# Filler matmuls in the head of a SwiGLU kernel: from two groups to three

## The chip, the cores and the metric

The kernel runs on one core of a Trainium2 chip. The metric is device time in microseconds (us) of one execution; a median of several is quoted, with the lowest and highest. "Span" is the time from the first to the last instruction in a profile; it is 1.3 to 1.4 us shorter than the device time of the same execution throughout.

## The reference

```python
B, S, D, F = 1, 2048, 640, 1536          # bf16
def reference(x, w_gate, w_up, w_down):
    g = silu(x @ w_gate)
    u = x @ w_up
    return (g * u) @ w_down
```

## The kernel before

The 2048 rows of x are done in four blocks of 512. For each block and each of twelve 128-wide slices of F, TensorE makes a gate projection `pg` and an up projection `pu`; ScalarE and VectorE make silu(pg)·pu; then the down projection follows. The first block needs x transposed, and this is done on TensorE, chunk by chunk (128 rows each, five transposes), in the order 0, 2, 1, 3. Chunks 0 and 2 are the first x pieces on the two DMA queues, 1 and 3 the second.

TensorE's matmuls follow each other slowly at first and about twice as fast later: in the profile before, 128 columns take 107 ns up to 3.47 us and 56 ns from 4.48 us on. I call this a low clock and the full one, although the column of the granted clock reads 1.00 throughout. With no fillers at all the change came at 7.0 to 7.4 us (the first experiment below). So the kernel fills TensorE with matmuls of ones ("fillers", into a tile `pw` that nobody reads) while it has nothing else to do:

```python
N_WARM = 20
W_CHUNKS = [(0, 1), (1, 3), (3, 6), (6, 9), (9, 12)]   # slices of F per weight load
...
for c in (0, 1):                                        # x: first pieces 0, 2; second 1, 3
    for i, eng in enumerate(queues):                    # queues: SyncE, ScalarE
        load_x(eng, c + 2 * i, c + 2 * i + 1)
for dst, src in ((wg_sb, wg_v), (wu_sb, wu_v)):         # then slice 0 of gate and up
    ...
load_w(nc.sync, wg_sb, wg_v, *W_CHUNKS[1])              # then slices 1 and 2, and so on
...
def warm(n):
    for _ in range(n):
        nc.tensor.matmul(pw[:, 0:P], lhsT=ones[:], rhs=ones[:], start=True, stop=True)
...
if sb == 0 and fc == 0:
    h = (SUB - 1) * P
    warm(N_WARM)
    for n, c in enumerate((0, 2, 1)):
        transpose_chunk(c, [(nc.vector.tensor_copy, ("po_a", "po_b")[n % 2], 0, KD)])
    transpose_chunk(SUB - 1, [...])                     # chunk 3: copies on VectorE and ScalarE
    warm(2)
    proj(pg, wg_sb, fc, sb, 0, h)                       # chunks 0 to 2: needs copy of chunk 1
    proj(pg, wg_sb, fc, sb, h, S_BLK)
    proj(pu, wu_sb, fc, sb, 0, S_BLK)
    keep_order(mybir.EngineType.PE)                     # TensorE keeps this order
```

## Time and profile before

| what | value |
|---|---|
| median of the first three runs | 164.19 us (164.17 to 164.63) |
| span of the profiled execution | 163.1 us (its device time: 164.41 us) |
| TensorE busy | 159.1 us, 98% |
| fillers | 22, 2.6 us busy |
| first gate matmul | 5.39 us after the start |

The lines themselves stand in the prediction. Two habits of reading matter here. A matmul's record is longer than its turn: most fillers have records of 311 ns and start 107 ns apart. What counts is the step from start to start. For 128 columns it is 107 ns at the low clock and 56 ns at the full one. And the moment at which the step changes is what I call the release of the clock.

### The profile page before, as it was taken

How to read it: one execution, taken by the hardware profiler on the slowest of the kernel's cores; microseconds unless marked ns; L12 is line 12 of the kernel's file. 1: busy time of each engine (PE TensorE's matmuls, PEld its weight loads, DVE VectorE, ACT ScalarE, POOL GpSimd, SP SyncE). 2: the span in 40 equal slices, each digit the busy share in tenths (PEclk: the TensorE clock that was granted, in tenths of full speed). 3: DMA queues.
4: the chain of work that ended last, by engine and by line, in shares of the span. 5: the costliest groups of instructions: out<-in, count | busy, mean ns of one | idle time of the engine just before them, and what ended most of it. 6: DMA issues, size and time to landing. Idle time of an engine off the chain costs nothing.

```text
span 163.1 us, 1864 instructions
## 1 busy us (share of the span) xinstructions
PE 159.1 (98%) x764; PEld 75.2 (46%) x779; DVE 37.8 (23%) x58; ACT 42.2 (26%) x71; POOL 0.6 (0%) x6
## 2 busy tenths in 40 slices
PE   8899999999999999999999999999999999999994
PEld 7544444444444444444444444444444444445442
DVE  2323333310013333311003333331001333332000
ACT  3222222212232222221222222221214222222121
POOL 1000000000000000000000000000000000000000
DMA  7999999803200000003110000000320000000312
GB/s 212 274 333 330 361 245 187 152 6 60 67 32 0 0 0 0 4 0 34 64 64 0 2 4 0 0 0 3 62 68 32 0 0 0 0 0 4 54 34 72
DMA packets 26888, 11.26 MB, mean 69 GB/s; under 512 B 17664, under 2 KB 26880, under 8 KB 26880
## 3 DMA queue, kind: packets, MB, share of 16 engines
q1 hardware_dynamic: 17968, 10.16, 22.9%
q10 hardware_dynamic: 8912, 0.98, 3.9%
q8 instruction: 6, 0.10, 0.3%
q14 instruction: 2, 0.02, 0.0%
HBM read 6.55 MB, written 2.62 MB: 56 GB/s over the span
## 4 chain that ended last, share of the span: by engine, by line
PE 95%; DMA 2%; issue 1%; DVE 0%; SPq 0%
PE pg L134 32%; PE pu L134 31%; PE po_a L204 25%; PE po_t L180 6%; DMA x_sb<-in_x_dram 2%; PE po_b L217 0%; PE pt L125 0%; DVE xT L130 0%; SPq L74 0%; DVE ot_b L225 0%
## 5 line engine op out<-in xcount | busy, mean ns | idle before, releaser
L134 PE MATMUL pg<-xT,wg_sb 128*128 128x512 bf16 (+2 forms) x245 | 59.7, 375 | 0.2 <-DVE xT L130 0.2
L134 PE MATMUL pu<-xT,wu_sb 128*128 128x512 bf16 x230 | 59.0, 379 | 0.5
L172 DVE TENSOR_TENSOR aT<-sg,pu 128x512 bf16<-128x512 f32 x48 | 33.0, 687 | 100.8 <-PE pu L134 100.8
L171 ACT ACTIVATE sg<-pg 128x512 f32<-128x512 f32 x48 | 28.7, 597 | 71.1 <-PE pg L134 71.1
L204 PE MATMUL po_a<-wd_sb,aT 128*128 128x512 bf16 x188 | 41.9, 379 | 0.2
L134 PEld LDWEIGHTS <-wg_sb 128*128 128x128 bf16 x245 | 23.8, 98 | 28.4 <-DMA wg_sb<-in_w_gate_dram 0.4
L134 PEld LDWEIGHTS <-wu_sb 128*128 128x128 bf16 x240 | 23.4, 98 | 28.1
L204 PEld LDWEIGHTS <-aT 128*128 128x128 bf16 x192 | 18.8, 98 | 22.5
L212 ACT CAST ot<-po_a 128x512 bf16<-128x512 f32 x16 | 9.4, 585 | 32.4 <-PE po_a L204 19.2
L180 PE MATMUL po_t<-aT,wd_sb 128*128 128x512 bf16 (+1 forms) x47 | 10.3, 366 | 0.1
L180 PEld LDWEIGHTS <-wd_sb 128*128 128x128 bf16 x48 | 4.7, 98 | 5.1
L189 ACT CAST ot_t<-po_t 128x512 bf16<-128x512 f32 (+1 forms) x4 | 2.2, 558 | 11.6 <-PE po_t L180 11.6
L190 DVE STREAM_TRANSPOSE ot_q<-ot_t 128x512 bf16<-128x512 bf16 (+1 forms) x4 | 2.7, 678 | 9.1 <-ACT ot_t L189 9.1
L103 PE MATMUL pw<-ones 128*128 128x128 bf16 x22 | 2.6, 302 | 0.4 <-DVE ones L78 0.4
L225 DVE CAST ot_b<-po_b 128x128 bf16<-128x128 f32 x1 | 0.3, 292 | 9.9 <-PE po_b L217 9.9
L125 PE MATMUL pt<-ident,x_sb 128*128 128x128 bf16 x20 | 2.0, 269 | 0.5 <-DMA x_sb<-in_x_dram 0.5
L130 DVE COPY xT<-pt 128x640 bf16<-128x640 bf16 (+1 forms) x4 | 1.7, 439 | 3.5 <-PE pt L125 3.5
L103 PEld LDWEIGHTS <-ones 128*128 128x128 bf16 x22 | 2.2, 139 | 0.4 <-DVE ones L78 0.4
L125 PEld LDWEIGHTS <-x_sb 128*128 128x128 bf16 x20 | 1.6, 122 | 0.9 <-DMA x_sb<-in_x_dram 0.8
L89 ACT ACT_TABLE_LOAD x1 | 1.3, 1283 | 2.0 <-issue 2.0
L130 ACT COPY xT<-pt 128x384 bf16<-128x384 bf16 x1 | 0.5, 479 | 1.6 <-PE pt L125 1.6
L217 PEld LDWEIGHTS <-aT 128*128 128x128 bf16 x12 | 0.8, 98 | 0.2
(9 smaller groups left out, 2.1 us busy)
## 6 DMA issues: line engine op xcount, KB each, us to landing
out_dram<-ot SPq DMA_DIRECT2D x16, 128.0 KB, 1.7
wd_sb<-in_w_down_dram SPq DMA_DIRECT2D x1, 1920.0 KB, 11.8
wg_sb<-in_w_gate_dram SPq DMA_DIRECT2D x3, 480.0 KB, 7.1
wu_sb<-in_w_up_dram SPq DMA_DIRECT2D x3, 480.0 KB, 7.8
out_dram<-ot_q ACTq DMA_DIRECT2D x12, 32.0 KB, 1.9
x_sb<-in_x_dram SPq DMA_DIRECT2D x2, 160.0 KB, 3.1
x_sb<-in_x_dram ACTq DMA_DIRECT2D x2, 160.0 KB, 3.3
wg_sb<-in_w_gate_dram SPq DMA_DIRECT2D x1, 320.0 KB, 4.3
```

Of the source, the lines that this page charges most:

```text
L89: nc.scalar.activation(silu_first[:], ones[:, 0:1], ACT.Silu)
L103: nc.tensor.matmul(pw[:, 0:P], lhsT=ones[:], rhs=ones[:], start=True, stop=True)
L125: nc.tensor.transpose(out=pt[:, kd - k0, :], in_=x_sb[:, c, kd * P : (kd + 1) * P], identity=ident[:],)
L130: copy(out=xT[:, k0:k1, c_sl], in_=pt[:])
L134: nc.tensor.matmul(ps[:, c0:c1], lhsT=w_sb[:, kd, fc * P : (fc + 1) * P], rhs=xT[:, kd, sb * S_BLK + c0 : sb * S_BLK + c1], start=(kd == 0 ...
L171: nc.scalar.activation(sg[:], pg[:], ACT.Silu)
L172: nc.vector.tensor_tensor(out=aT[:, fc, s_sl], in0=sg[:], in1=pu[:], op=ALU.mult)
L180: nc.tensor.matmul(po_t[:], lhsT=wd_sb[:, kf, DA:D], rhs=aT[:, kf, sb * S_BLK : sb * S_BLK + n_t], start=(kf == 0), stop=(kf == KF - 1),)
L189: nc.scalar.copy(ot_t[:], po_t[:])
L190: nc.vector.transpose(out=ot_q[:], in_=ot_t[:])
L204: nc.tensor.matmul(po_a[:], lhsT=aT[:, kf, s0 : s0 + P], rhs=wd_sb[:, kf, 0:DA], start=(kf == 0), stop=(kf == KF - 1),)
L212: nc.scalar.copy(ot[:], po_a[:])
```

## The change

Its intent: spread the fillers over the head so that TensorE is kept busy in its holes too. Two fewer at the front, four new ones between the two pairs of x pieces, and four instead of two before the gate projection.

```diff
-    N_WARM = 20
+    N_WARM, N_GAP = 18, 4
@@
                     transpose_chunk(
                         c, [(nc.vector.tensor_copy, ("po_a", "po_b")[n % 2], 0, KD)]
                     )
+                    if c == 2:
+                        warm(N_GAP)
@@
-                warm(2)
+                warm(N_GAP)
                 proj(pg, wg_sb, fc, sb, 0, h)
```

## The prediction

> **What bounds the kernel now.** I read four things, in this order: the page for the whole, the chain of waits over the first 10 us for the head, the timeline of the head for the gaps on TensorE, and the table of stretches for how much of each gap is idle.
>
> The page first. Its slices, its chain and the group of the fillers:
>
> ```profile
> PE   8899999999999999999999999999999999999994
> PE 95%; DMA 2%; issue 1%; DVE 0%; SPq 0%
> L103 PE MATMUL pw<-ones 128*128 128x128 bf16 x22 | 2.6, 302 | 0.4 <-DVE ones L78 0.4
> ```
>
> TensorE is busy in every slice except the first two and the last, and 95% of the chain that ends last is its matmuls. The change touches nothing but the first slices (40 slices over 163.1 us are 4.08 us each), so whatever it does must happen before about 6 us. The fillers are 22 matmuls of ones, 2.6 us busy in all. The only other engine in this chain worth a per cent is the DMA, 2% of 163.1 us, or some 3.3 us, and that is at the head.
>
> The chain of waits over the first 10 us, in order of time, says which thing in the head is on the path:
>
> ```profile
> 0.46 3.81 DMA x_sb<-in_x_dram
> 4.26 0.05 issue
> 4.31 0.51 PE pt L125 x5
> 4.82 0.02 issue
> 4.84 0.50 DVE xT L130
> 5.35 0.04 issue
> 5.39 1.25 PE pg L134 x10
> ```
>
> The reader is to see that no filler is in it, and neither is the first half of x. The path is: the last of the second x pieces lands at 4.26, its five transposes take 0.51, VectorE copies them in 0.50, and the gate projection starts at 5.39. After that TensorE runs without a gap that matters.
>
> The timeline of the head shows where the fillers stand beside that path (start, length, engine, line, what):
>
> ```profile
> 0.40 2.31 PE L103 MATMUL pw<-ones 128*128 128x128 bf16 x20 [0.40 <-DVE ones L78]
> 2.51 1.27 PE L125 MATMUL pt<-ident,x_sb 128*128 128x128 bf16 x10
> 4.31 0.78 PE L125 MATMUL pt<-ident,x_sb 128*128 128x128 bf16 x10 [0.53 <-DMA x_sb<-in_x_dram]
> 4.92 0.27 PE L103 MATMUL pw<-ones 128*128 128x128 bf16 x2
> 5.37 1.09 PEld L134 LDWEIGHTS <-wg_sb 128*128 128x128 bf16 x10 [0.35 <-DMA wg_sb<-in_w_gate_dram]
> 5.39 1.25 PE L134 MATMUL pg<-xT,wg_sb 128*128 128x384 bf16 x10 [0.19 <-DVE xT L130]
> ```
>
> There are two holes: 0.53 us before the second x pieces, and 0.19 us before the gate projection. The gate projection has two releasers close together: its weight load was let go by the landing of the gate slice, at 5.37, and its first matmul by VectorE's copy, at 5.39. Removing one of the two would leave the other.
>
> These lines also hold the clock. A matmul's record runs on past the start of the next by its pipeline, so I take the step from start to start. Twenty fillers in 2.31 us with a last record of 0.31 us (the source view of their line gives 311 ns as the median) make 2.00/19 = 105 ns a step. The last two fillers, 0.27 us with a last record of 0.22, step by about 55 ns. The single records of the transposes say when this changes: they step by 107 ns up to 3.47, and by 80, 87 and then 56 ns from 4.31 on. So in this execution the clock was released between about 4.3 and 4.5 us, just as the second x pieces came, and before the gate projection. The column of the granted clock reads 1.00 throughout and doesn't show it.
>
> Last, the table of stretches, cut at the joints of the head, gives the idle share:
>
> ```profile
> 3.57:4.30 0.73, 0.21 (x2) 0.00 (x0) 0.69 (x2) 0.00 (x0) 0.00 (x0) 1.00 1.02 230
> 5.03:5.38 0.35, 0.17 (x3) 0.01 (x1) 0.35 (x2) 0.26 (x1) 0.00 (x0) 1.00 0.96 267
> ```
>
> In the first stretch TensorE started nothing; the 0.21 us is the tail of two earlier records. So counted by starts the first hole is 0.73 us and the second 0.35 us. The DMA column is full: the transfers are what is waited for.
>
> [...]the x pieces here took 2.5 to 3.9 us from issue to landing (the tile view of x_sb)[...].
>
> **The change part by part.**
>
> First, two fillers fewer at the front. They would end 2 x 0.107 = 0.21 us earlier, so that TensorE could take the first transpose at 2.51 - 0.21 = 2.30. But the landings in the trace have the last part of the first x piece at 2.46, and the first weight load from x started at 2.50, 0.10 later than it would have behind a filler. It waited for the landing already. So the first transposes stay at 2.50 and a gap of 0.2 us opens ahead of them: 0.00 us on the path.
>
> Second, four fillers after the first two chunks. The last of those ten transposes starts at 3.47, so the fillers start at 3.57 and at the slow step take 4 x 0.107 = 0.43 us, to 4.00. The second pieces land at 4.26. There is 0.26 us to spare, and no filler takes a buffer that the transposes need (pw is its own tile, and they wait for no other engine): 0.00 us on the path. Were the clock released in this hole they would be shorter still.
>
> Third, four instead of two before the gate projection: two more, at the released step 2 x 0.056 = 0.11 us. The transposes' slots end at 4.92, and four fillers to 5.15. The gate slice's landing lets the load go at 5.37, the copy lets the matmul go at 5.39: 0.22 us to spare, and 0.00 us on the path.
>
> Sum in the state of the traced execution: 0.00. TensorE does four matmuls more, 26 against 22, all in holes. If anything comes of the change, it comes through the clock[...].
>
> **The rivals.**
>
> (a) The clock is released earlier, or more surely. For it: in the traced execution the release comes just at the edge where it begins to matter[...]. In executions with a later release, five transposes at 107 instead of about 60 ns a step put the copy, and so the gate projection, some 0.2 to 0.25 us later, and each microsecond of projections at half clock costs 0.5 us more. That is the size of the 164.63 us run, 0.45 us above the others. Against it: two of three runs lie at 164.18, and those have nothing to win[...]. If only the late executions win, the median stays; if all had a part, some 0.2 us, it would be 164.0.
>
> (b) The fillers get in the way. In an execution where the clock is still slow at 5 us, ten transposes from 4.31 end their slots at 4.31 + 10 x 0.107 = 5.38, two fillers bring it to 5.59 and four to 5.81. The copy would release the gate projection at about 4.31 + 4 x 0.107 + 0.31 + 0.05 + 0.49 + 0.05 = 5.65. So two fillers hide, and four delay it by 0.16 us. For it: nothing shows that such executions are rare. [...]It would make 164.35 of a late execution's 164.19, if one had that time, and hardly move the median.
>
> (c) The transfers move. Weights for the second slice land at 7.19 and their first load starts at 7.34, so even a head that was 0.2 us faster would meet this wait after 0.15 us. This caps any win. The DMA issues themselves stay in their order on SyncE and ScalarE; the landing of the second x pieces was set by one late part of sixteen (fifteen had landed by 3.29, the last at 4.26), which can well differ by some tenths between executions, with the change or without.
>
> **Range and chances.** I give 0.7 to no effect (164.19), 0.2 to (a) in a form that the median shows (164.0), 0.1 to (b) (164.35). The mean is 164.17, and as the last case is mostly hidden by a median I say 164.15 us. The spread of the kernel before, 0.46 us in three runs, is wider than all of this, so the range is set by it: 163.90 (the whole cap of (c) and some luck with the landings) to 164.60 (a median caught in the late state). Two per cent is 3.3 us, nearly the whole time before the second x pieces land; no part of the change reaches that either way. Faster 0.01, within 2% 0.98, slower 0.01.
>
> **What would show it.** In the profile after: 18 fillers, then the first transposes still at about 2.5 with a wait for x_sb now named ahead of them; four fillers at about 3.6 that end their slots at about 4.0; the idle time before the second transposes cut from 0.53 to some 0.1 us and still put down to the x transfer; four fillers at about 4.9; the gate projection released by VectorE's copy or the gate slice, within 0.2 us of 5.39 after correction for the landing. It would be wrong if the transposes of the second pieces start later than 0.1 us after their landing, if the gate projection follows a filler without a gap, or if the gate projection starts over 0.3 us earlier at the same landing, which would mean that the clock had been on the path in most executions.

Cut from the recorded text is what no trace or run of this case shows: a section on when the clock is released, two arguments of (a) and one of (b) about the same, a remark on the transfers of x, and the end of the paragraph on the sum. The forecast stands without them. Its sum is 0.00 us on the path, from three parts of 0.00 us each, and its time comes from the three chances: 0.7 x 164.19 + 0.2 x 164.0 + 0.1 x 164.35 = 164.17 us, said as 164.15. The term cut from the sum was a count of idle time, 0.43 + 0.11 - 0.21 = 0.33 us less of it on TensorE, and that this moves the release was not shown. The 0.5 us for each microsecond of projections at the low clock is my estimate, from the steps of 107 and 56 ns.

## The result

The kernel after took 164.23 us in the median of six runs (163.98 to 164.82), beside 164.28 us (164.16 to 164.63) for six of the kernel before. The ratio of the two is 0.9997, with a 95% interval of 0.9976 to 1.0018: the same. A ratio here is the mean time of one kernel's fast runs over that of the other's of the same rounds, so it is not quite the ratio of the medians.

The profile after tells a less smooth story, for it caught the slowest of the six, at 164.82 us. From its page, the chain by engine and the group of the fillers:

```profile
PE 96%; DMA 2%; issue 1%; SPq 0%; DVE 0%
L103 PE MATMUL pw<-ones 128*128 128x128 bf16 x26 | 3.2, 304 | 0.4 <-DVE ones L78 0.4
```

Four fillers more, as the diff says, 26 of them. From the chain of waits in the first 10 us of the kernel after (start, length, what; its ends are left out):

```profile
0.46 3.91 DMA x_sb<-in_x_dram
4.37 0.04 issue
4.41 1.25 PE pt L125 x10
5.66 0.28 PE pw L103 x4
5.93 1.09 PE pg L134 x10
```

Here a filler is in the chain: the gate projection follows ten transposes and four fillers without a wait. The timeline of TensorE in the same execution (start, length, what, and in brackets the idle time before it):

```profile
0.40 2.10 PE L103 MATMUL pw<-ones 128*128 128x128 bf16 x18 [0.40 <-DVE ones L78]
2.45 1.25 PE L125 MATMUL pt<-ident,x_sb 128*128 128x128 bf16 x10
3.49 0.63 PE L103 MATMUL pw<-ones 128*128 128x128 bf16 x4
4.41 1.25 PE L125 MATMUL pt<-ident,x_sb 128*128 128x128 bf16 x10 [0.29 <-DMA x_sb<-in_x_dram]
5.45 0.48 PE L103 MATMUL pw<-ones 128*128 128x128 bf16 x4
5.77 1.25 PE L134 MATMUL pg<-xT,wg_sb 128*128 128x384 bf16 x10
```

The second ten transposes take 1.25 us, where they took 0.78 us before: they ran at the low clock. The single records put the release between 5.5 and 5.7 us, over a microsecond later than in the profile before (4.3 to 4.5). The gate projection starts at 5.77 instead of 5.39 us, and the span is 163.5 instead of 163.1 us: the same 0.4 us. The table of stretches confirms that the holes were filled (length, then TensorE's busy time):

```profile
3.57:4.30 0.73, 0.55 (x6) 0.29 (x3) 0.61 (x2) 0.00 (x0) 0.00 (x0) 1.00 1.25 283
5.03:5.38 0.35, 0.35 (x6) 0.35 (x5) 0.22 (x1) 0.00 (x0) 0.00 (x0) 1.00 1.06 271
```

So the fillers did what they were placed for, TensorE was busier (0.21 to 0.55 us, and 0.17 to 0.35 us), and this execution was released later all the same. Is that the change, or chance? That is what the experiments had to tell.

### The profile page after: what moved, and what is told of

It reads as the page before. It is cut to its first block, busy times and chain, and to the rows that moved or that the text cites. A ratio compares the mean times of both kernels' runs of the same rounds, so it can differ in the third digit from the quotient of the medians.

```text
span 163.5 us, 1872 instructions
## 1 busy us (share of the span) xinstructions
PE 159.9 (98%) x768; PEld 76.0 (46%) x783; DVE 37.9 (23%) x58; ACT 42.2 (26%) x71; POOL 0.6 (0%) x6
## 4 chain that ended last, share of the span: by engine, by line
PE 96%; DMA 2%; issue 1%; SPq 0%; DVE 0%
PE pg L134 32%; PE pu L134 31%; PE po_a L206 25%; PE po_t L182 6%; DMA x_sb<-in_x_dram 2%; PE pt L125 1%; PE po_b L219 0%; SPq L74 0%; DVE ot_b L227 0%; PE pw L103 0%
## 5 line engine op out<-in xcount | busy, mean ns | idle before, releaser
L103 PE MATMUL pw<-ones 128*128 128x128 bf16 x26 | 3.2, 304 | 0.4 <-DVE ones L78 0.4
L103 PEld LDWEIGHTS <-ones 128*128 128x128 bf16 x26 | 2.7, 145 | 0.4 <-DVE ones L78 0.4
L125 PE MATMUL pt<-ident,x_sb 128*128 128x128 bf16 x20 | 2.5, 311 | 0.3 <-DMA x_sb<-in_x_dram 0.3
```

The lines of the kernel that those rows point to most:

```text
L125: nc.tensor.transpose(out=pt[:, kd - k0, :], in_=x_sb[:, c, kd * P : (kd + 1) * P], identity=ident[:],)
```

## The experiments

**Theory:** The fillers at the front are what brings the release forward; those in the holes neither move it nor the path, and what differs between executions is the moment of release and the landings. **Rival (a):** the busy time in the holes makes the release earlier or surer. **Rival (b):** fillers in the holes stand in TensorE's order ahead of real work and cost. All variants below but one, the wide slices, change only the three counts, written (front, first hole, before the gate projection): the kernel before is (20, 0, 2), the kernel after (18, 4, 4). Each was timed six times beside eleven runs of the kernel before; each group of four has its own chip, so a variant is compared with the kernel before of its own group. Those had medians of 164.26, 164.14 and 164.29 us in the first, second and third group of four below. Where an expectation names a range in which the release should fall, the range rests on no trace; what was measured stands below it.

### First group: what the fillers do at all

No fillers, (0, 0, 0), made from the kernel after as the other variants of the counts are:

```diff
-N_WARM, N_GAP = 18, 4
+N_WARM, N_GAP, N_END = 0, 0, 0
@@
-                warm(N_GAP)
+                warm(N_END)
```

> No fillers at all. Theory (the fillers only buy an earlier release of the clock, the rest of the head waits for transfers): the first transposes stay at 2.4 to 2.5 us and the second ones at 4.3 to 4.4, because landings set them, but the release, 4.4 us in the profile before and about 5.6 in the profile after, moves to 6 to 9 us; the second ten transposes step by 107 ns, the gate projection starts at about 5.65 and runs at half speed until the release, so the time rises by 0.25 plus half of 0.4 to 3.4 us: 164.7 to 166.2 us, most likely 165.3. Rival (the fillers do nothing, all is in the landings): 164.2 us and a release below 6 us.[...]

Measured: 165.27 us median (164.83 to 166.88), ratio 1.0076 (1.0043 to 1.0109). The release came between 7.0 and 7.4 us. The timeline of TensorE in this run:

```profile
2.42 2.36 PE L125 MATMUL pt<-ident,x_sb 128*128 128x128 bf16 x20 [2.42 <-DMA x_sb<-in_x_dram]
4.93 2.32 PE L134 MATMUL pg<-xT,wg_sb 128*128 128x384 bf16 x10
```

Ten gate matmuls take 2.32 us instead of 1.25: they ran at the low clock. The gate projection itself started earlier than in the profile before, 4.93 against 5.39 us, because the x pieces and the gate slice happened to land earlier (chunk 1 at 3.49 us against 4.26, the first part of the gate slice at 4.88 against 5.33). The theory holds: the fillers are worth about 1.25 us in the mean (165.53 us here and 164.28 us for the kernel before in these rounds; 1.0 us by the medians, as one run took 166.88 us), and through the clock: nothing else in the head came later. The release came 2.1 to 2.5 us after the first gate matmul and 4.6 to 5.0 us after the first transpose. How much work a release needs, and of which kind, no run here shows, so this stays open.

Front fillers taken away, the others of the kernel after kept, (0, 4, 4):

> None at the front, four in the first hole and four before the gate projection. Theory: the front ones are what starts the activity 2 us early; without them the release falls in 5.5 to 9 us, and the eight others change that little: 164.7 to 166 us, like the kernel with none, 0.1 to 0.2 us better or worse. Rival (it is the holes that count): close to 164.2 us, release below 5.6 us.

Measured: 165.18 us median (164.47 to 165.61), ratio 1.0050 (1.0026 to 1.0073), release between 7.3 and 7.5 us. From its timeline:

```profile
5.53 2.20 PE L134 MATMUL pg<-xT,wg_sb 128*128 128x384 bf16 x10
```

Again most of the gate projection ran at the low clock. The eight fillers in the holes do not replace the front ones. They may have spared a little against none at all (means 165.10 and 165.53 us), but most of that difference is one run at 166.88 us.

The first-hole fillers added alone, (20, 4, 2), and the front cut alone, (18, 0, 2):

> The kernel before with the four fillers in the first hole added alone (20, 4, 2). Theory: they end their slots at about 4.0, before the second x pieces land at 4.3, so nothing on the path moves: within 0.2 us of the kernel before. Rival (a) (they make the release earlier or surer): 0.2 us faster or more, and the spread of runs under 0.2 us. Rival (a second cost): over 0.2 us slower.

> The kernel before with two fillers fewer at the front alone (18, 0, 2). Theory: the first transposes still wait for the landing at 2.4 to 2.5 us with a hole of about 0.2 us ahead of them; same time within 0.2 us. Rival[...]: the hole pushes the release later in some runs, 0.2 us or more slower, slowest runs above 164.8 us.

Measured: 164.41 us (164.15 to 164.73), ratio 1.0007 (0.9991 to 1.0023), and 164.51 us (164.04 to 164.64), ratio 1.0008 (0.9992 to 1.0024). Both are level with the kernel before within their intervals. Their profiles were worth more than their times: in the front-cut run the clock was released between 5.8 and 6.1 us, as late as in the profile after, in a kernel that has no fillers in the first hole:

```profile
4.65 0.42 PE L103 MATMUL pw<-ones 128*128 128x128 bf16 x2
4.90 1.83 PE L134 MATMUL pg<-xT,wg_sb 128*128 128x384 bf16 x10
```

Here only two fillers stood before the gate projection. Their slots ended at 4.86, and it still waited for VectorE's copy of chunk 1, which ended at 4.85.

### Second group: the place before the gate projection, and more executions

Four instead of two before the gate projection alone, (20, 0, 4):

> The kernel before with four fillers instead of two before the gate projection alone (20, 0, 4). Theory: with an early release (about 4.4 us) they end 0.2 us before the copy lets the gate projection go, with a late one (5.6 us and more) two more slow ones cost up to 0.16 us; in the mean 0 to 0.1 us slower than the kernel before. Rival (they make the release surer): 0.2 us faster or more.

Measured: 164.20 us (163.92 to 164.61), ratio 0.9998 (0.9982 to 1.0015). No effect in the mean. Its profile caught a late release (5.5 to 5.8 us), and there the delay can be seen:

```profile
5.15 0.61 PE L103 MATMUL pw<-ones 128*128 128x128 bf16 x4
5.58 1.28 PE L134 MATMUL pg<-xT,wg_sb 128*128 128x384 bf16 x10
```

VectorE's copy of chunk 1 ended at 5.35, yet the gate projection started at 5.58, behind the fillers. In the profile before it had followed the copy by 0.05 us, so about 0.18 us was due to TensorE's own order.

Twenty more fillers in that place, (18, 4, 24):

> The kernel after with 24 fillers before the gate projection, to make the cost of that place visible. Theory (fillers there stand in TensorE's order ahead of the gate projection, and are free only up to the copy and the gate slice): 20 more at 56 to 107 ns each are 1.1 to 2.1 us, of which 0 to 0.25 us hide; the second gate slice would start about 1 us later, 8.5 to 9.2 us; 165.1 to 165.6 us. Rival (fillers are free wherever they stand, as the head waits for transfers): below 164.6 us.

Measured: 165.18 us (165.03 to 167.85), ratio 1.0054 (1.0039 to 1.0069). The timeline of TensorE:

```profile
3.86 1.10 PE L125 MATMUL pt<-ident,x_sb 128*128 128x128 bf16 x10
4.80 1.50 PE L103 MATMUL pw<-ones 128*128 128x128 bf16 x24
6.14 1.25 PE L134 MATMUL pg<-xT,wg_sb 128*128 128x384 bf16 x10
```

The gate projection waits for the 24 fillers, 4.80 + 24 x 0.056 = 6.14 us. Fillers were not free in this place: the chain of waits has all 24 of them, 1.34 us, right ahead of the gate projection, and VectorE's copy not at all. The second gate slice started at 8.31 us, less late than the 8.5 to 9.2 I had written, as the release was early (4.5 to 4.7 us). The one run at 167.85 us counts as slow, as it is over 1.5% above the fastest of its kernel, and is not in the ratio; the granted clock for it is 1.0 like the others', no profile caught such an execution, and it is not explained.

The kernel after again:

> The kernel after once more, for more executions and a second profile. Theory (no effect; the moment of release and the landings spread both kernels alike): mean within 0.15 us of the kernel before in the same rounds, runs from 163.9 to 164.8 us; the span minus the start of the second gate slice again 155.5 us. Rival (a): mean 0.2 us faster or more. Rival (b): mean 0.15 us slower or more.

Measured: 164.61 us (164.22 to 165.04), ratio 1.0021 (1.0004 to 1.0039). The mean is 0.36 us above that of the kernel before. This is more than the theory allowed, it meets the mark set for rival (b), 0.15 us or more, and it was the reason for the third group. Its profile again caught the slowest of the six, with a release between 6.1 and 6.3 us.

A trial aimed at the other cap, the landing of the second gate slice, on the kernel before:

```diff
-W_CHUNKS = [(0, 1), (1, 3), (3, 6), (6, 9), (9, 12)]
+W_CHUNKS = [(0, 2), (2, 4), (4, 6), (6, 9), (9, 12)]
-    eng.dma_start(out=dst[:, k0:k1, wslice(0, 1)], in_=src[:, k0:k1, wslice(0, 1)])
+    eng.dma_start(out=dst[:, k0:k1, wslice(*W_CHUNKS[0])], in_=src[:, k0:k1, wslice(*W_CHUNKS[0])])
```

> The kernel before, fillers untouched, with the first weight slices two columns of blocks wide instead of one (the slices then are 0-2, 2-4, 4-6, 6-9, 9-12). Theory that the landing of the second gate slice (6.9 to 7.8 us in the five profiles so far, first used at 7.3 to 7.9) caps what any filler can win: with it gone the second gate slice is never waited for, and the runs become 0 to 0.3 us faster in the mean, if the wider first slice doesn't land later than about 5.4 us. Rival (the first slice has twice the bytes and lands later, which delays the gate projection itself): slower by 0.2 us or more, first gate matmul after 5.7 us.

Measured: 165.22 us (164.80 to 167.09), ratio 1.0098 (1.0051 to 1.0144). A miss. The timeline:

```profile
5.20 0.66 PE L134 MATMUL pg<-xT,wg_sb 128*128 128x384 bf16 x3 [0.61 <-DMA wg_sb<-in_w_gate_dram]
6.17 0.78 PE L134 MATMUL pg<-xT,wg_sb 128*128 128x384 bf16 x7 [0.31 <-DMA wg_sb<-in_w_gate_dram]
7.47 1.03 PE L134 MATMUL pu<-xT,wu_sb 128*128 128x512 bf16 x4 [0.52 <-DMA wu_sb<-in_w_up_dram]
```

The first slice, twice as large, landed in two parts at 5.15 and 6.13 us, and the up slice at 7.19, so TensorE waited three times. The rival won, though not by the sign it named (a first gate matmul after 5.7 us; it started at 5.20 and the rest of the projection waited until 6.17): the narrow first slice is better in this head than one of twice the width, although it leaves a cap behind it.

### Third group: how much is chance

The kernel before against itself, and the kernel after a third time:

> The kernel before unchanged, timed as if it were a changed one: a null control, for the size of what six runs against eleven can show by chance, and a second profile of it. Theory (executions differ by the moment of release and by landings, both by chance): mean within 0.15 us of the other runs of the kernel before. If it differs by 0.3 us or more, then the 0.3 us by which the kernel after fell behind in the last rounds need no cause in the change. In the profile the release may fall anywhere between 3.9 and 6.9 us, and the span minus the start of the second gate slice is 155.5 us.

> The kernel after a third time: its first six runs were level with the kernel before, the second six 0.3 us slower. Theory (no effect): within 0.15 us, and the three sets together within 0.15 us. Rival (b) (the two added fillers before the gate projection cost in executions with a late release): 0.1 us slower in the mean, as two slow fillers before a release that stays where it is take 0.11 us of work at full speed from what follows. A third 0.3 us would say that something else in the change costs.

Measured: the copy 164.32 us (164.15 to 164.61), ratio 1.0006 (0.9985 to 1.0028); the kernel after 164.29 us (164.11 to 164.68), ratio 1.0008 (0.9984 to 1.0031). The two are level, and one of the eleven runs of the kernel before took 165.05 us, as much as the slowest of the kernel after. So the 0.36 us of the second group did not repeat. The control by itself doesn't show that chance makes so much: it differed from its eleven runs by 0.09 us in the mean.

The two profiles are a lucky pair, close in their landings: second x pieces down at 3.28 and 3.26 us for chunk 1, the second gate slice at 7.26 and 7.19 us. The timeline of the copy of the kernel before:

```profile
2.50 1.82 PE L125 MATMUL pt<-ident,x_sb 128*128 128x128 bf16 x20
4.16 0.27 PE L103 MATMUL pw<-ones 128*128 128x128 bf16 x2
4.72 1.26 PE L134 MATMUL pg<-xT,wg_sb 128*128 128x384 bf16 x10 [0.29 <-DMA wg_sb<-in_w_gate_dram]
7.31 1.25 PE L134 MATMUL pg<-xT,wg_sb 128*128 128x512 bf16 x5 [0.25 <-DMA wg_sb<-in_w_gate_dram]
```

And of the third profile of the kernel after:

```profile
3.49 0.62 PE L103 MATMUL pw<-ones 128*128 128x128 bf16 x4
3.92 0.76 PE L125 MATMUL pt<-ident,x_sb 128*128 128x128 bf16 x10
4.98 1.25 PE L134 MATMUL pg<-xT,wg_sb 128*128 128x384 bf16 x10
7.24 1.25 PE L134 MATMUL pg<-xT,wg_sb 128*128 128x512 bf16 x5
```

In the kernel before all twenty transposes run in one row: there is no first hole, as the second pieces were there in time. In the kernel after the four fillers stand in that row, and the gate projection starts 0.26 us later, 4.98 against 4.72 us. (The pair is not alike in the release, which came at 3.8 to 4.0 us against 3.5, the latter earlier than the 3.9 to 6.9 us I had expected, so not all of this need be the fillers' doing.) Yet the second gate slice starts at 7.31 and 7.24 us, in both just after its weights landed (the first step of it in the records is 226 to 227 ns instead of 216, as after a wait). That delay was hidden behind the transfer.

The kernel after with two fillers before the gate projection, (18, 4, 2), and the kernel before with none there, (20, 0, 0):

> The kernel after with the two added fillers before the gate projection taken back (18, 4, 2). Theory (no effect): within 0.15 us of the kernel after and of the kernel before. Rival (b): level with the kernel before, 0.1 us or more faster than the kernel after of the same rounds. If the hole at the front and the fillers in the first hole cost something together: as slow as the kernel after.

> The kernel before without the two fillers before the gate projection (20, 0, 0). Theory (the fillers there stand ahead of the gate projection and buy nothing): 0 to 0.1 us faster than the kernel before, nothing slower. Rival (they keep the clock released, or make the release surer): 0.2 us or more slower, or runs above 165.5 us[...].

Measured: 164.20 us (163.99 to 164.50), ratio 0.9998 (0.9976 to 1.0021), and 164.34 us (164.02 to 164.70), ratio 1.0006 (0.9984 to 1.0028). Neither differs from the kernel before by more than the copy does. In the mean (18, 4, 2) took 164.23 us and (18, 4, 4) 164.34 us, which has the sign of rival (b) and the size of chance.

### All profiles side by side

The start of the second gate slice on TensorE tells everything that came of the head: the span minus that start is 155.5 to 155.6 us in all fourteen profiles, whatever the fillers. Landing and release come from the trace's single records.

| kernel (front, hole, end) | chunk 1 of x landed | release | first gate matmul | second gate slice starts | span |
|---|---|---|---|---|---|
| before (20, 0, 2) | 4.26 | 4.3–4.5 | 5.39 | 7.56 | 163.1 |
| before, copy | 3.28 | 3.5 | 4.72 | 7.31 | 162.8 |
| after (18, 4, 4) | 4.37 | 5.5–5.7 | 5.77 | 7.94 | 163.5 |
| after, again | 4.28 | 6.1–6.3 | 5.79 | 8.16 | 163.7 |
| after, third | 3.26 | 3.8–4.0 | 4.98 | 7.24 | 162.8 |
| (20, 4, 2) | 3.44 | 4.3–4.5 | 5.29 | 7.67 | 163.2 |
| (18, 0, 2) | 3.33 | 5.8–6.1 | 4.90 | 7.65 | 163.2 |
| (20, 0, 4) | 4.06 | 5.5–5.8 | 5.58 | 7.77 | 163.3 |
| (18, 4, 2) | 3.57 | 3.8–4.0 | 4.97 | 7.13 | 162.7 |
| (20, 0, 0) | 4.19 | 3.5–4.2 | 5.27 | 7.44 | 163.0 |
| (18, 4, 24) | 3.72 | 4.5–4.7 | 6.14 | 8.31 | 163.9 |
| (0, 0, 0) | 3.49 | 7.0–7.4 | 4.93 | 8.22 | 163.7 |
| (0, 4, 4) | 3.43 | 7.3–7.5 | 5.53 | 8.65 | 164.2 |
| wide slices (20, 0, 2) | 3.33 | 3.8–4.0 | 5.20 | 8.33 | 163.9 |

With fillers at the front the release falls anywhere from 3.5 to 6.3 us, early and late in kernels with and without fillers in the first hole. It was after 5 us in three of the six profiles with 18 at the front and in one of the six with 20; so few can't tell whether the two fewer make it later, a rival that no experiment here settles. By the times it is not seen: (18, 0, 2) was level with the kernel before. Chunk 1 of x lands anywhere from 3.26 to 4.37 us. In the kernel before and in (20, 0, 0), both late, fifteen of its sixteen parts were down by 3.29 and 3.11 us, and one part came a microsecond later. And three rows, the copy of the kernel before, the third of the kernel after and (20, 4, 2), have the second gate slice waiting for its own weights.

Over all its 18 runs the kernel after took 164.41 us in the mean, and the 28 runs of the kernel before in the same rounds 164.28 us. The difference is 0.13 us, with a standard error of 0.09 us: a cost of that size is possible and not shown. No variant beat both kernels; the best row above, (18, 4, 2), owes its 162.7 us to an early release and early landings.

## Why the prediction was right

The time, "same", and the sum of about zero came out: 164.15 us was forecast and 164.23 us measured. That the median came so close is partly luck, as the second six runs of the same kernel had one of 164.61 us, just above the range. Its steps fared differently.

- **The bound and the place to look: right.** What follows the second gate slice's start took 155.5 to 155.6 us in every profile.
- **Front fillers, "0.00 us on the path": right.** The first transposes of the kernel after started at 2.45, 2.29 and 2.45 us, at or just after a landing (or, in the second, as soon as the eighteen were through), and the hole ahead of them cost nothing. That the front fillers bring the release forward, and that the eight in the holes don't replace them, was shown by (0, 0, 0) and (0, 4, 4), released at 7.0 to 7.4 and 7.3 to 7.5 us.
- **First-hole fillers, "0.26 us to spare": true of one kind of execution only.** I read one landing, 4.26 us, as if it were the kernel's. Of the six profiles with fillers both at the front and in the first hole, four had chunk 1 down by 3.72 us or earlier, and the fillers, which end their slots at 3.9 to 4.1, then stood in the row of transposes. In the lucky pair the gate projection came 0.26 us later, hidden only because the second gate slice's transfer ended later still. There the zero was right by luck, for a reason that I had named elsewhere, as the cap (c).
- **The cap (c): named, but mis-sized.** I took the 0.15 us from the landing, 7.19, to the start of the weight load, 7.34. But that load ran ahead of its matmul, which started at 7.56. In the lucky pair the first matmul followed the landing by 0.05 us, so by my estimate the head had 7.56 - 7.24 = 0.32 us to win.
- **End fillers, "0.22 us to spare": right after an early release, wrong after a late one.** This is rival (b). In the late executions the gate projection followed the fillers; against the end of VectorE's copy plus 0.05 us it was late by 0.07 us (after: copy over at 5.65, gate at 5.77), 0.18 us (after, again: 5.56 and 5.79) and 0.18 us in (20, 0, 4). I had estimated 0.16 us. But not all of it need reach the end: if the release stays where it is, two fillers at the low clock take from the work behind them only what they are worth at the full clock, by my estimate 2 x 56 ns = 0.11 us at most. I had overlooked that. No run separates so small a cost from chance.
- **Rival (a), an earlier or surer release: nothing for it was seen.** The release lay at about 5.6, 6.2 and 3.9 us in the three profiles of the kernel after, and at about 4.4 and 3.5 us in the two of the kernel before. Three and two are too few to exclude a small shift either way.
- **The signs that I named.** One of those of failure did occur, a gate projection that follows a filler without a gap. It marks late executions with four fillers in that place; with two, in (18, 0, 2), the copy still set the start. Two signs of success were missed in the first profile after: the idle time before the second transposes fell to 0.29 and not to about 0.1 us, and the gate projection came 0.27 us later than 5.39 after correction for the landing, outside the 0.2 us. The spread of the profiles is explained by the table: two times, a landing and a release, each with about a microsecond or more of play, and a third, the second slice's transfer, that cuts off the gain of the luckiest executions.

What stays open: the rare runs 1.6 us and more above their kernel's median, one of (0, 0, 0), two of the wide slices, and the slow one of (18, 4, 24). None was caught in a profile. For one of the wide slices' two, 167.09 us, the granted clock is 0.99; for the others it is 1.0.

## What to carry to other kernels

A profile is one execution: before counting spare time against a transfer's landing or the release of the clock, take several profiles of the same kernel and see how far those move. Here chunk 1 of x landed anywhere from 3.26 to 4.37 us, and with 18 or 20 fillers at the front the release fell anywhere from 3.5 to 6.3 us. A filler ahead of real work in TensorE's order was free here only in executions in which that work would have waited anyway: in the profile before, two fillers ended their slots at 5.03 us and the gate projection waited for the copy until 5.39; in that of (18, 4, 24) the gate projection followed the fillers at 6.14 us, and the ratio was 1.0054. When a head has three limits close together, look for one late instant that sums them up, here the start of the second gate slice (155.5 to 155.6 us before the end in all fourteen profiles), and compare kernels by it.
